# Reordered beginning of a one-core attention + MLP + expert kernel: cumulative-sum rows, value scaling, second head's maxima, table load and pair transfers

## The chip, the cores and the metric

The program runs on one core of a Trainium2 chip. The time is the device time of one execution in microseconds; the number to be forecast is the median over several executions.

## What is computed

Three stages follow each other. The first is causal attention with a decay over 4 batches x 8 heads, 576 positions and head dimension 64; the second a mixing and MLP block; the third an expert block with attention per expert. The change touches the first stage and its overlap with the second. Cut to that:

```python
# q, k, v: (4, 8, 576, 64), f: (4, 8, 576)
log_f = np.log(np.clip(f, 0.0001, 1.0))
cum = np.cumsum(log_f, axis=-1)
scores = scale * np.matmul(q, k.transpose(0, 1, 3, 2)) + (cum[..., :, None] - cum[..., None, :])
scores = np.where(causal, -1000000000.0, scores)
attn = np.exp(scores - np.max(scores, axis=-1, keepdims=True))
attn_out = (attn / (attn.sum(-1, keepdims=True) + 1e-09)) @ v
# second stage, x = heads of attn_out side by side, (4, 576, 512)
u = x + (xt @ U @ V).transpose(0, 2, 1)
y = u + np.maximum(u @ w_ch1, 0.0) @ w_ch2
```

## The kernel before

**Heads and pairs.** Heads go two by two: pair p holds heads 2p and 2p+1, and a batch is four pairs. `load_pair(p)` transfers q and k (`qkt`) and v (`vr`) from DRAM; `split_high(p)` casts q and k on ScalarE into the tiles `qa`, `ka` of the first head and `qb`, `kb` of the second; `split_low(p)` transfers the row of cumulative sums into rows 64 and 65 of `ka`, copies between the tiles by DMA, and subtracts the casts on GpSimd. There are two sets of head tiles, used by pairs in turn, and from pair 4 on one tile `qkt` and one `vr`.

**Per head.** `row_max` multiplies q by k into `ua` and `ub`, takes masked maxima on VectorE into the five columns of `mx`, turns `mx` on TensorE into `mt`, subtracts a constant into `mr` on VectorE, and sends `mr` by two DMAs (L186, L187) into row 66 of `qa`. Here this is called the row of that head. `scores` then multiplies all 67 rows into `sc` in two parts (u = 0, 1), takes the exponential on ScalarE (`pf`, L222), casts it (`ph`, L223), and subtracts on VectorE (`pl`, L224). `weighted_values` multiplies `ph`, `pl` by the values' parts `vh`, `vl`. The tiles `ua`, `ub`, `sc` share one PSUM pool of two buffers.

**Values.** `values(p)` is a generator in three steps: the absolute maximum `am` of `vr` (L251); its transpose `amt` and the power of two `ar` (L256 to L258); then the broadcast `rsp`, its reciprocal `rs` (L265), the scaling of `vr` (L270), the cast `vh` (L271) and the subtraction `vl` (L272).

**Cumulative sums.** `log_sums` reads f, takes Ln on ScalarE, scans on VectorE and leaves two rows per head in `chl`. It stores all of `chl` into `cdram` (L490). Pair 0 takes its rows from `chl`, all others read `cdram` (L548).

**First batch.** `first_batch` goes over heads h = 0 to 7. With the scores of head h go the maxima of head h+2, the row of head h+1, the weighted values of head h-1, and, where h is odd, the transfers of the pair after next (`next_inputs(p + 2)`). `mix(p)` forms `gp` and `g` (TensorE, ScalarE, VectorE L591), then `up` on TensorE, and stores the result for the MLP.

**Weights of the MLP.** `load_quarter_steps` reads pieces of the weights (`raw`), narrows them in three VectorE steps L308, L310, L311 with one ScalarE step L309 between the first two (into `wst`, one buffer), casts on ScalarE (L359, `w1h` or `w2h`) and subtracts on GpSimd (L360, `w1l` or `w2l`). A quarter has four pieces of `w1` and four of `w2`. `ffn_out` (L414) uses all four `w2` pieces of its quarter in each of its sums. MLP work is filled in between the heads from pair 5 on.

**What sets the order.** TensorE's instructions stand in the order of the code. On the other engines a scheduler orders the instructions when the program is built. Each engine then works through its list in that order; SyncE's list (SP) is the queue from which nearly all DMAs are issued. A DMA also waits on a completion count that an earlier DMA used.

The line numbers are those of the profile of before.

Of the kernel before, what the change touches and what calls it, by code (L numbers as in the profile page):

```python
# [8 lines left out]
F32 = mybir.dt.float32  # L9
# [5 lines left out]
AF = mybir.ActivationFunctionType  # L15
OP = mybir.AluOpType
# [3 lines left out]
B, H, S, D = 4, 8, 576, 64  # L20
# [15 lines left out]
PSCALE_LN = 8.0 * math.log(2.0)  # L36
# [9 lines left out]
ISC = 0.125  # L46
# [8 lines left out]
def f32(ap):  # L55
    return ap.bitcast(F32)
# [3 lines left out]
def kernel(  # L60
# [13 lines left out]
    nc = tc.nc  # L74
# [4 lines left out]
    def pool(name, bufs=1, side="left", space=None):  # L79
        kw = {} if space is None else {"space": space}  # L80
        if space is None:
            kw["side"] = side
            kw["reuse_waits"] = "tile"
        return tc.alloc_tile_pool(name=name, bufs=bufs, **kw)
# [6 lines left out]
    small = pool("small", 4)  # L91
# [43 lines left out]
    cdram = dram.tile([B * H, 2, S], F32, name="cdram")  # L135

    cur = {}
# [5 lines left out]
    def drain(gen):  # L143

        while True:
            try:
                next(gen)
            except StopIteration as end:
                return end.value

    def row_max(hb, mx, apart=False):


        qa, qb, ka, kb = hb
        ua = ps2.tile([P, 2, 512], F32, name="ua", tag="s2")
        for c0, c1 in ((0, HC), (HC, S)):
            nc.tensor.matmul(ua[:, c0 // HC, 0:HC], qa[0:66, M_LO[4]:S], ka[0:66, c0:c1],
                             start=True, stop=True)
        nc.vector.tensor_tensor_reduce(
            ua[:, :, 0:HC], ua[:, :, 0:HC],  # L160
            maskm[:].rearrange("p (c n) -> p c n", c=2), 1.0, NEG, OP.add, OP.max, mx[:, 4:5])
        if apart:
            yield
        ub = ps2.tile([P, 2, 512], F32, name="ub", tag="s2")
        where = {3: (0, 0), 0: (0, 448), 2: (1, 0), 1: (1, 320)}
        for t in (3, 2, 1, 0):
            bk, off = where[t]
            w = M_W[t]
            n = 64 if t == 0 else P
            nc.tensor.matmul(ub[0:n, bk, off:off + w], qa[0:66, M_LO[t]:M_LO[t] + n],  # L170
                             ka[0:66, 0:w], start=True, stop=True)
        for t in (3, 2, 1, 0):
            bk, off = where[t]
            w = M_W[t]
            n = 64 if t == 0 else P
            m0 = S - P if t == 0 else S - w
            nc.vector.tensor_tensor_reduce(  # L177
                ub[0:n, bk, off:off + w], ub[0:n, bk, off:off + w], maskm[0:n, m0:m0 + w], 1.0, NEG,
                OP.add, OP.max, mx[0:n, t:t + 1])
        yield  # L180
        mt = psf.tile([NT, P], F32, name="mt", tag="f")
        nc.tensor.transpose(mt[:], mx[:], ident[:])
        mr = small.tile([NT, P], F32R, name="mr", bufs=2)
        nc.vector.tensor_scalar(mr[:], mt[:], PSCALE_LN / ISC, None, OP.subtract)
        row = f32(qa[66:67, :])
        nc.sync.dma_start(row[:, 0:64], f32(mr[0:1, 0:64]))  # L186
        cur["last"] = nc.sync.dma_start(row[:, 64:S].rearrange("o (t p) -> o t p", p=P),  # L187
                                        f32(mr[1:NT, :]))
# [59 lines left out]
    def value_scale(vr):  # L248

        am = small.tile([P, 1], F32, name="am")  # L250
        nc.vector.tensor_reduce(am[:], vr, AX.XYZ, OP.max, apply_absolute_value=True)  # L251
        yield
        at_ = psf.tile([1, P], F32, name="amt", tag="f")
        nc.tensor.transpose(at_[:], am[:], ident[:])
        ar = small.tile([1, 1], F32, name="ar")
        nc.vector.tensor_reduce(ar[:], at_[:], AX.X, OP.max)  # L256
        nc.vector.tensor_scalar(ar[:], ar[:], 1.0e-30, None, OP.max)
        nc.vector.tensor_scalar(ar[:].bitcast(I32), ar[:].bitcast(I32), 0x7F800000, None,  # L258
                                OP.bitwise_and)
        yield  # L260

        rp = psf.tile([P, 1], F32, name="rsp", tag="f")
        nc.tensor.matmul(rp[:], ones1[:], ar[:].bitcast(BF16)[:, 1:2], start=True, stop=True)
        rs = small.tile([P, 1], F32, name="rs")
        nc.vector.reciprocal(rs[:], rp[:])  # L265
        return rs
# [209 lines left out]
    def log_sums():  # L476

        pa = cur["fu"].tile([P, 2, S], F32, name="pa", tag="uh")
        pb = cur["fu"].tile([P, 2, S], F32, name="pb", tag="ul")
        chl = cur["fu"].tile([P, 2, S], F32R, name="chl", tag="uh")  # L480
        fr, ones, cum = pa[0:B * H, 0, :], pa[0:B * H, 1, :], pb[0:B * H, 0, :]
        nc.sync.dma_start(fr, f)
        nc.vector.memset(ones, 1.0)
        nc.vector.tensor_scalar(fr, fr, 1.0e-4, 1.0, OP.max, OP.min)
        nc.scalar.activation(fr, fr, AF.Ln)
        nc.vector.tensor_tensor_scan(cum, ones, fr, 0.0, OP.mult, OP.add)
        nc.vector.tensor_scalar(chl[0:B * H, 0, :], cum, -1.0 / ISC, None, OP.mult)
        nc.vector.scalar_tensor_tensor(chl[0:B * H, 1, :], cum, -1.0 / ISC,
                                       f32(chl[0:B * H, 0, :]), OP.mult, OP.subtract)
        nc.sync.dma_start(cdram[:], f32(chl[0:B * H]))  # L490
        return chl

    cur["sums"] = log_sums()
# [20 lines left out]
    def pair_heads(p):  # L514
        return heads[2 * (p % 2)], heads[2 * (p % 2) + 1]
# [23 lines left out]
    def split_low(p):  # L539
        if p >= NPAIR:  # L540
            return
        qkt, vr = st_in[p]
        (qa, qb, ka, kb), (qa2, qb2, ka2, kb2) = pair_heads(p)
        tq, tk = qkt[:, 0, :], qkt[:, 1, :]
        for j in range(2):
            hb = pair_heads(p)[j]
            src = f32(cur["sums"][j:j + 1]) if p == 0 else cdram[2 * p + j]
            nc.sync.dma_start(f32(hb[2][64:66, 0:S]), src)  # L548
        nc.sync.dma_start(f32(qa2[lo_, :]), f32(qb2[hi_, :]))
        nc.sync.dma_start(f32(ka2[lo_, :S]), f32(kb2[hi_, :S]))  # L550
        nc.sync.dma_start(f32(qb[lo_, :]), f32(qa[lo_, :]))
        nc.sync.dma_start(f32(kb[hi_, :S]), f32(ka[lo_, :S]))
        nc.sync.dma_start(f32(kb2[lo_, :S]), f32(kb2[hi_, :S]))
        nc.gpsimd.tensor_tensor(qb[hi_, :], tq[lo_], f32(qa[lo_, :]), OP.subtract)
        nc.gpsimd.tensor_tensor(kb[lo_, :S], tk[lo_], f32(ka[lo_, :S]), OP.subtract)
        nc.gpsimd.tensor_tensor(qb2[lo_, :], tq[hi_], f32(qb2[hi_, :]), OP.subtract)
        nc.gpsimd.tensor_tensor(kb2[hi_, :S], tk[hi_], f32(kb2[hi_, :S]), OP.subtract)

    def values(p):
        if p >= NPAIR:  # L560
            return
        vr = st_in[p][1]
        st_rs[p] = yield from value_scale(vr[:])
        value_parts(vr[:], st_rs[p], *vhs[p % 2])

    def maxima(p, j, apart=False):
        if p < NPAIR:
            yield from row_max(pair_heads(p)[j], next_mx(), apart)

    def one(gen):  # L570

        next(gen, None)
# [50 lines left out]
    load_pair(0)  # L623
    split_high(0)
    split_low(0)
    del cur["sums"]
    drain(values(0))
    drain(maxima(0, 0))
    m_first = maxima(0, 1)
    one(m_first)  # L630
    load_pair(1)
    split_high(1)
    split_low(1)
# [57 lines left out]
    def next_inputs(p):  # L691
        load_pair(p)
        split_high(p)
        split_low(p)

    def pair_scores(p, j):
        st_p[p, j] = yield from scores(pair_heads(p)[j])

    def first_batch(m_next):

        mixing = vals = iter(())
        for h in range(2 * NP):
            p, j = divmod(h, 2)
            sc = pair_scores(p, j)
            m_last, m_next = m_next, maxima(p + 1, j, True)
            one(sc)
            one(m_next)
            if j == 0:  # L710
                xs[p] = sx.tile([P, NT, P], F32, name="x", bufs=2)
                vals = values(p + 1)
                one(vals)
            one(sc)
            one(m_last)
            if j == 1:
                next_inputs(p + 2)
            one(m_next)
            if j == 1:
                one(vals)  # L720
            if h > 0:
                attend(*divmod(h - 1, 2))
            if j == 0:
                one(vals)
                one(mixing)
            elif p > 0:
                mixing = mix(p - 1)
                one(mixing)
            if j == 1:
                weights_after(p)  # L730
        one(mixing)
        return m_next
# [475 lines left out]
```

## Time and profile before

| | |
|---|---|
| median of 3 runs | 910.22 us (908.41 to 911.0) |
| the profiled execution's own time | 908.8 us |
| its span, first to last instruction | 906.9 us |
| TensorE busy (PE) | 835.0 us, 92% |
| VectorE busy (DVE) | 540.5 us, 60% |
| ScalarE busy (ACT) | 431.3 us, 48% |
| GpSimd busy (POOL) | 298.7 us, 33% |
| mean granted TensorE clock | 0.967 |

A row of a timeline gives the start in us, the duration in us, the engine, the line, the operation, what it writes and reads, its shape, and in brackets how long its engine sat idle before it and who ended that idle time. SPq is the queue of SyncE, so its durations are those of issuing a DMA and not of the transfer. Rows of windows give busy time and number of instructions of each engine in a stretch, then the granted clock (1.00 is 2.4 GHz, 0.50 is 1.2 GHz), the share of the DMA engines and GB/s.

### The profile page before, as it was taken

What the parts mean: (1) busy time and instruction counts of PE and PEld (TensorE: products, weight loads), DVE (VectorE), ACT (ScalarE), POOL (GpSimd) and SP (SyncE); (2) the same over time, 40 slices, a digit from 0 to 9 for tenths busy, and PEclk for the clock granted to TensorE, in tenths of its full rate; (3) what the DMA queues carried; (4) which work ended last, traced back from release to release, by engine and by line L of the source; (5) the groups of instructions that cost most, each with busy time, mean ns of one, the idle gap of its engine ahead of it and who ended that gap; (6) DMA issues with size and microseconds to landing.
All of it is one profiled execution on the core that took longest, in us unless ns stands there. A gap on an engine that the chain in (4) does not pass through costs nothing.

```text
span 906.9 us, 19020 instructions
## 1 busy us (share of the span) xinstructions
PE 835.0 (92%) x7476; PEld 782.0 (86%) x7476; DVE 540.5 (60%) x1464; ACT 431.3 (48%) x836; POOL 298.7 (33%) x283
## 2 busy tenths in 40 slices
PE   2796798998999999989999999999999999989997
PEld 2685687887899989989999999999999898989775
DVE  6789887886676666642234443222223777787654
ACT  3667565565444554342145543322211575665553
POOL 9446464444423433011135243513202241311000
PEclk9989577999999999999999999999999999999998
DMA  6335465354333432103159663433203231311222
GB/s 189 110 102 163 136 198 168 108 155 121 123 114 88 134 109 59 42 15 119 53 185 330 218 223 116 120 108 116 80 26 92 54 86 40 87 41 35 73 89 71
DMA packets 68809, 101.94 MB, mean 112 GB/s; under 512 B 6640, under 2 KB 49456, under 8 KB 68720
## 3 DMA queue, kind: packets, MB, share of 16 engines
q1 hardware_dynamic: 64448, 92.47, 34.1%
q10 hardware_dynamic: 4272, 8.26, 2.6%
q8 instruction: 59, 0.97, 0.4%
q14 instruction: 30, 0.25, 0.1%
HBM read 60.33 MB, written 22.56 MB: 91 GB/s over the span
## 4 chain that ended last, share of the span: by engine, by line
PE 70%; DVE 13%; DMA 6%; ACT 6%; issue 3%; SPq 1%; POOL 1%; DVEq 0%; ACTq 0%; POOLq 0%
PE cps L414 19%; PE hps L399 18%; PE sc L213 8%; PE pq L913 4%; PE po L1025 3%; DVE pl L224 3%; PE pv L978 3%; PE av L240 3%; DVE ub L177 2%; PE ub L170 2%; PE gp L587 2%; DMA ust<-udram 2%; PE av L244 2%; PE av L242 2%; DMA vr<-in_v_dram 2%
## 5 line engine op out<-in xcount | busy, mean ns | idle before, releaser
L414 PE MATMUL cps<-hh,w2h 128*128 128x288 f32 x512 | 154.8, 303 | 4.7 <-ACT w2h L359 2.0
L224 DVE TENSOR_TENSOR pl<-pf,ph 128x576 f16<-128x576 f32 x144 | 122.8, 855 | 51.5 <-ACT ph L223 51.3
L414 PE MATMUL cps<-hh,w2l 128*128 128x288 f32 x512 | 151.3, 296 | 1.0 <-POOL w2l L360 1.0
L414 PE MATMUL cps<-hl,w2h 128*128 128x288 f32 x512 | 150.5, 294 | 0.0
L399 PE MATMUL hps<-uh,w1h 128*128 128x288 f32 x512 | 144.8, 304 | 0.1
L404 DVE SCALAR_TENSOR_TENSOR hl<-hps,hh 128x288 fp32r<-128x288 f32 x128 | 58.3, 455 | 140.6 <-ACT hh L403 140.5
L399 PE MATMUL hps<-uh,w1l 128*128 128x288 f32 x512 | 141.4, 298 | 0.0
L403 ACT ACTIVATE hh<-hps 128x288 fp32r<-128x288 f32 x128 | 52.4, 410 | 156.8 <-PE hps L399 156.6
L414 PEld LDWEIGHTS cps<-hh,w2h 128*128 128x128 f32 x512 | 96.3, 188 | 6.7 <-ACT w2h L359 2.7
L222 ACT ACTIVATE pf<-sc 128x576 f32<-128x576 f32 x144 | 83.8, 612 | 37.2 <-PE sc L213 34.6
L399 PEld LDWEIGHTS hps<-uh,w1h 128*128 128x128 f32 x512 | 97.4, 190 | 0.8 <-DVE yc L416 0.5
L399 PEld LDWEIGHTS hps<-uh,w1l 128*128 128x128 f32 x512 | 97.6, 191 | 0.0
L414 PEld LDWEIGHTS cps<-hh,w2l 128*128 128x128 f32 x512 | 96.2, 188 | 1.2 <-POOL w2l L360 1.2
L414 PEld LDWEIGHTS cps<-hl,w2h 128*128 128x128 f32 x512 | 96.2, 188 | 0.0
L223 ACT CAST ph<-pf 128x576 f16<-128x576 f32 x144 | 89.2, 637 | 1.5
L213 PE MATMUL sc<-qa,ka 67*128 67x288 f32 (+4 forms) x288 | 77.0, 327 | 13.7 <-DMA qa<-mr 6.9
L240 PE MATMUL av<-vh,ph 128*128 128x65 f16 x720 | 87.0, 202 | 1.5 <-DVE x L287 1.5
L399 PE MATMUL hps<-ul,w1h 128*128 128x288 f32 x512 | 88.3, 295 | 0.0
L177 DVE CUSTOM_DVE_ANT_0 ub<-ub,maskm 128x448 f32<-128x448 f32 x192 | 81.3, 424 | 8.5 <-PE ub L170 7.5
L242 PE MATMUL av<-vl,ph 128*128 128x64 f16 x720 | 85.7, 198 | 0.0
L244 PE MATMUL av<-vh,pl 128*128 128x65 f16 x720 | 85.4, 198 | 0.0
L240 PEld LDWEIGHTS <-ph 128*128 128x128 f16 x720 | 68.5, 101 | 9.9 <-DVE x L287 1.7
(182 smaller groups left out, 1955.2 us busy)
## 6 DMA issues: line engine op xcount, KB each, us to landing
raw<-in_w_dram SPq DMA_DIRECT2D x32, 512.0 KB
ust<-udram SPq DMA_DIRECT2D x20, 576.0 KB
qkt<-in_qk_dram SPq DMA_DIRECT2D x16, 576.0 KB
yc<-ydram SPq DMA_DIRECT2D x14, 576.0 KB
ydram<-yc SPq DMA_DIRECT2D x14, 576.0 KB
vr<-in_v_dram SPq DMA_DIRECT2D x16, 320.0 KB
udram<-ustage ACTq DMA_DIRECT2D x16, 288.0 KB
ydram<-ust SPq DMA_DIRECT2D x8, 576.0 KB
```

The costliest lines, as they stand in the source:

```text
L177: nc.vector.tensor_tensor_reduce(ub[0:n, bk, off:off + w], ub[0:n, bk, off:off + w], maskm[0:n, m0:m0 + w], 1.0, NEG, OP.add, OP.max, mx[0 ...
L213: nc.tensor.matmul(ps[:, bk, off:off + w], wa, xa, start=bk not in banks[:n], stop=bk not in banks[n + 1:])
L222: nc.scalar.activation(pfv, view, AF.Exp, scale=ISC)
L223: nc.scalar.copy(ph[:, o0:o0 + n], pf[:, 0:n])
L224: nc.vector.tensor_tensor(pl[:, o0:o0 + n], pf[:, 0:n], ph[:, o0:o0 + n], OP.subtract)
L240: nc.tensor.matmul(av[0:m, it, :], ph[0:k, c:c + m], vh[0:k, jt, :], start=first, stop=False)
L242: nc.tensor.matmul(av[0:m, it, 0:64], ph[0:k, c:c + m], vl[0:k, jt, :], start=False, stop=False)
L244: nc.tensor.matmul(av[0:m, it, :], pl[0:k, c:c + m], vh[0:k, jt, :], start=False, stop=last)
L399: nc.tensor.matmul(ph[:], wa[:, k, fs], xa[:, k, :], start=n == 0, stop=n == 3 * KT - 1)
L403: nc.scalar.activation(hh[:], ph[:], AF.Relu)
L404: nc.vector.scalar_tensor_tensor(hl[:], ph[:], 0.0, f32(hh[:]), OP.max, OP.subtract)
L414: nc.tensor.matmul(pc[:], wa[:, t, dsl], xa[:], start=n == 0, stop=n == 3 * FT - 1)
```

## The change

It has five edits. The store of `chl` into `cdram` leaves `log_sums` and is issued after the DMA that brings pair 0's second row of sums into `ka` (kept as `cur["row"]`). A one-column exponential, `soon`, follows the Ln, so that the exponential's table is loaded there. Of `values(0)` only the first two steps stand ahead of the maxima; its third step, and the first step of head 1's maxima, stand behind head 0's `mr` (kept as `cur["mr"]`). In `first_batch` the transfers, casts and copies of `next_inputs(p + 2)` may issue their SyncE instructions only after the row that was the last one issued when head h began.

```diff
-        nc.vector.tensor_scalar(mr[:], mt[:], PSCALE_LN / ISC, None, OP.subtract)
+        cur["mr"] = nc.vector.tensor_scalar(mr[:], mt[:], PSCALE_LN / ISC, None, OP.subtract)
...
+        soon = small.tile([B * H, 1], F32, name="soon", bufs=1)
...
         nc.scalar.activation(fr, fr, AF.Ln)
+        nc.scalar.activation(soon[:], fr[:, 0:1], AF.Exp)
...
-        nc.sync.dma_start(cdram[:], f32(chl[0:B * H]))
         return chl
...
-            nc.sync.dma_start(f32(hb[2][64:66, 0:S]), src)
+            cur["row"] = nc.sync.dma_start(f32(hb[2][64:66, 0:S]), src)
...
     split_low(0)
+    with tc.issue_after(cur["row"].ins):
+        nc.sync.dma_start(cdram[:], f32(cur["sums"][0:B * H]))
     del cur["sums"]
-    drain(values(0))
+    v_first = values(0)
+    one(v_first)
+    one(v_first)
     drain(maxima(0, 0))
     m_first = maxima(0, 1)
-    one(m_first)
+    with tc.issue_after(cur["mr"].ins):
+        one(m_first)
+    with tc.issue_after(cur["mr"].ins):
+        one(v_first)
     load_pair(1)
...
             sc = pair_scores(p, j)
+            row = cur["last"]
...
             if j == 1:
-                next_inputs(p + 2)
+                with tc.issue_after(row.ins):
+                    next_inputs(p + 2)
```

`issue_after(x)` orders each instruction of its block that runs on the engine of x behind x on that engine, without a semaphore.

On SyncE the queue of the beginning stood so before: the store, pair 0's rows of sums, copies, pair 1's rows out of `cdram`, copies, then head 0's row.

```order
L490 DMA cdram<-chl 32x1152
L548 DMA ka_137<-chl 2x1x576
L548 DMA ka_145<-chl 2x1x576
L549 DMA qa_143<-qb_144 64x576
L553 DMA kb_146<-kb_146 64x576
L548 DMA ka_153<-cdram 2x576
L549 DMA qa_159<-qb_160 64x576
L552 DMA kb_154<-ka_153 64x576
L553 DMA kb_162<-kb_162 64x576
L186 DMA qa_135<-mr 1x16x4
L187 DMA qa_135<-mr 1x4x128
L524 DMA vr<-in_v_dram 128x640
```

Now the store stands five places later, two copies ahead of the reads of `cdram`, which stand three and four places ahead of head 0's row:

```order
L549 DMA ka_138<-chl 2x1x576
L549 DMA ka_146<-chl 2x1x576
L554 DMA kb_147<-kb_147 64x576
L628 DMA cdram<-chl 32x1152
L550 DMA qa_160<-qb_161 64x576
L551 DMA ka_162<-kb_163 64x576
L549 DMA ka_154<-cdram 2x576
L549 DMA ka_162<-cdram 2x576
L552 DMA qb_153<-qa_152 64x576
L553 DMA kb_155<-ka_154 64x576
L186 DMA qa_136<-mr 1x16x4
L187 DMA qa_136<-mr 1x4x128
```

The store moved behind the rows of sums that it preceded, and closer to those that read it; the last copy for pair 1 moved behind head 0's row, and pair 2's `vr` further back.

On VectorE, at head 7, `g` of pair 2 stood before at the end of this stretch; `wst` is the second weight piece:

```order
L265 RECIPROCAL rs_1228<-rsp_1226 128x1
L270 TENSOR_SCALAR vr_922<-vr_922,rs_1228 128x640
L308 TENSOR_SCALAR wst_1295<-raw_1017 128x512
L224 TENSOR_TENSOR pl_1156<-pf_1184,ph_1155 128x512
L177 ISA ub_1217,mx2_96<-ub_1217,maskm_82 64x64
L224 TENSOR_TENSOR pl_1156<-pf_1188,ph_1155 128x512
L278 TENSOR_SCALAR den_1279<-av_1233,rs_950 128x5
L310 SCALAR_TENSOR_TENSOR wst_1295<-raw_1017,wst_1295 128x512
L311 SCALAR_TENSOR_TENSOR wst_1295<-raw_1017,wst_1295 128x512
L287 TENSOR_TENSOR x_1042<-av_1233,rn_1281 128x5x64
L591 TENSOR_TENSOR g_1290<-gp_1284,g_1290 32x128
```

Now:

```order
L224 TENSOR_TENSOR pl_1158<-pf_1165,ph_1157 128x576
L265 RECIPROCAL rs_1230<-rsp_1228 128x1
L310 SCALAR_TENSOR_TENSOR wst_1297<-raw_1019,wst_1297 128x512
L270 TENSOR_SCALAR vr_924<-vr_924,rs_1230 128x640
L278 TENSOR_SCALAR den_1281<-av_1235,rs_952 128x5
L311 SCALAR_TENSOR_TENSOR wst_1297<-raw_1019,wst_1297 128x512
L224 TENSOR_TENSOR pl_1158<-pf_1186,ph_1157 128x512
L224 TENSOR_TENSOR pl_1158<-pf_1190,ph_1157 128x512
L592 TENSOR_TENSOR g_1292<-gp_1286,g_1292 32x128
L177 ISA ub_1219,mx2_96<-ub_1219,maskm_82 64x64
L287 TENSOR_TENSOR x_1044<-av_1235,rn_1283 128x5x64
```

The piece's first step moved out of the stretch to a place ahead of it, and the last maximum and `x` moved behind `g`.

On VectorE, at pair 5, the eighth weight piece (the last of `w2` of the first quarter, `wst_1643`) stood before ahead of the two last `pl` of a head:

```order
L404 SCALAR_TENSOR_TENSOR hl_1867<-hps_1853,hh_1866 128x288
L308 TENSOR_SCALAR wst_1643<-raw_1634 128x512
L591 TENSOR_TENSOR g_1876<-gp_1870,g_1876 32x128
L310 SCALAR_TENSOR_TENSOR wst_1643<-raw_1634,wst_1643 128x512
L311 SCALAR_TENSOR_TENSOR wst_1643<-raw_1634,wst_1643 128x512
L224 TENSOR_TENSOR pl_1836<-pf_1892,ph_1835 128x512
L224 TENSOR_TENSOR pl_1836<-pf_1896,ph_1835 128x512
L308 TENSOR_SCALAR wst_1654<-raw_1650 128x512
L416 TENSOR_TENSOR ust_1550<-cps_1919,ust_1550 128x288
```

Now the seventh piece (`wst_1638`) stands there, and the eighth (`wst_1645`) behind them:

```order
L404 SCALAR_TENSOR_TENSOR hl_1869<-hps_1855,hh_1868 128x288
L308 TENSOR_SCALAR wst_1638<-raw_1627 128x512
L592 TENSOR_TENSOR g_1878<-gp_1872,g_1878 32x128
L310 SCALAR_TENSOR_TENSOR wst_1638<-raw_1627,wst_1638 128x512
L311 SCALAR_TENSOR_TENSOR wst_1638<-raw_1627,wst_1638 128x512
L224 TENSOR_TENSOR pl_1838<-pf_1894,ph_1837 128x512
L224 TENSOR_TENSOR pl_1838<-pf_1898,ph_1837 128x512
L308 TENSOR_SCALAR wst_1645<-raw_1636 128x512
L310 SCALAR_TENSOR_TENSOR wst_1645<-raw_1636,wst_1645 128x512
L311 SCALAR_TENSOR_TENSOR wst_1645<-raw_1636,wst_1645 128x512
L308 TENSOR_SCALAR wst_1656<-raw_1652 128x512
L416 TENSOR_TENSOR ust_1552<-cps_1921,ust_1552 128x288
```

From the fifth piece to the eighth, each stands about one place of a piece later; the ninth is where it was, so that from there on the lists of VectorE agree but for neighbours. On TensorE only the first 14 instructions changed places.

## Rows read from the trace of the kernel before

**Rows 1.** Windows, the first 20 us, and 144 to 154; columns as told above.

```profile
0.00:20.00 20.00, 4.47 (x16) 3.25 (x16) 13.25 (x34) 7.66 (x11) 18.18 (x41) 1.00 0.64 178
...
144.00:154.00 10.00, 9.39 (x71) 8.44 (x72) 9.54 (x24) 4.60 (x8) 4.02 (x3) 0.50 0.54 173
```

**Rows 2.** Timeline, SyncE's queue; columns as told above.

```profile
1.26 0.41 SPq L522 DMA_DIRECT2D qkt<-in_qk_dram  x1
...
7.28 0.58 SPq L490 DMA_DIRECT2D cdram<-chl  x1
...
11.59 0.58 SPq L548 DMA_DIRECT2D ka<-cdram  x2
...
17.54 0.56 SPq L186 DMA_DIRECT2D qa<-mr  x1
...
18.87 0.44 SPq L640 DMA_DIRECT2D ur<-in_u_dram  x1
```

**Rows 3.** Timeline, VectorE, the beginning.

```profile
10.44 0.82 DVE L251 TENSOR_REDUCE am<-vr 128x1 f32<-128x640 f32 x1 [1.47 <-DMA vr<-in_v_dram]
...
11.37 1.38 DVE L270 TENSOR_SCALAR vr<-vr,rs 128x640 f32<-128x640 f32 x1
12.68 0.75 DVE L159 CUSTOM_DVE_ANT_0 ua<-ua,maskm 128x576 f32<-128x576 f32 x1
...
17.24 0.27 DVE L184 TENSOR_SCALAR mr<-mt 5x128 fp32r<-5x128 f32 x1
...
21.35 1.45 DVE L308 TENSOR_SCALAR u<-ur 128x160 int32<-128x160 int32 x1 [2.59 <-DMA ur<-in_u_dram]
...
28.18 0.28 DVE L184 TENSOR_SCALAR mr<-mt 5x128 fp32r<-5x128 f32 x1 [1.55 <-PE mt L182]
```

**Rows 4.** Timeline, TensorE, the first scores of head 0.

```profile
19.99 0.58 PE L213 MATMUL sc<-qa,ka 67*128 67x288 f32 x1 [3.12 <-DMA qa<-mr]
```

**Rows 5.** Timeline, ScalarE: first cast, first exponential, pair 2's cast.

```profile
5.35 0.67 ACT L534 CAST qa<-qkt 64x576 fp32r<-64x576 f32 x1 [1.13 <-DMA qkt<-in_qk_dram]
...
22.83 0.34 ACT L309 ACTIVATE ur<-ur 128x160 f32<-128x160 f32 x1 [9.31 <-DVE u L308]
23.19 1.28 ACT L222 ACT_TABLE_LOAD   x1
24.49 0.65 ACT L222 ACTIVATE pf<-sc 128x576 f32<-128x576 f32 x1
...
27.40 0.67 ACT L534 CAST qa<-qkt 64x576 fp32r<-64x576 f32 x1 [1.56 <-PE sc L213]
```

**Rows 6.** Timeline, VectorE and TensorE, up to the wait for pair 2's g.

```profile
86.88 1.34 DVE L308 TENSOR_SCALAR wst<-raw 128x512 int32<-128x512 int32 x1
88.15 1.83 DVE L224 TENSOR_TENSOR pl<-pf,ph 128x512 f16<-128x512 f32 x1
...
94.03 0.58 PE L596 MATMUL up<-vs,g 96*128 96x256 f32 x1 [8.47 <-DVE g L591]
```

**Rows 7.** Timeline, all engines, around the first sum of `ffn_out`.

```profile
140.56 0.62 ACT L359 CAST w2h<-wst 128x512 fp32r<-128x512 f32 x1
...
141.32 1.26 POOL L360 TENSOR_TENSOR w2l<-wst,w2h 128x512 fp32r<-128x512 f32 x1 [0.69 <-ACT w2h L359]
141.73 2.00 DVE L224 TENSOR_TENSOR pl<-pf,ph 128x512 f16<-128x512 f32 x2 [2.36 <-ACT ph L223]
142.63 0.40 PE L414 MATMUL cps<-hh,w2l 128*128 128x288 f32 x1 [1.01 <-POOL w2l L360]
...
143.65 0.41 DVE L308 TENSOR_SCALAR wst<-raw 128x512 int32<-128x512 int32 x1
...
144.10 0.66 ACT L309 ACTIVATE raw<-raw 128x512 f32<-128x512 f32 x1 [1.89 <-DVE wst L308]
...
144.79 0.69 DVE L310 SCALAR_TENSOR_TENSOR wst<-raw,wst 128x512 int32<-128x512 int32 x1
...
145.52 1.80 DVE L311 SCALAR_TENSOR_TENSOR wst<-raw,wst 128x512 int32<-128x512 int32 x1
```

## The prediction

> **What bounds the kernel now.** I read the page first, then windows of each stretch, then the timelines. Over the whole run TensorE is busy 92%, but the change touches stretches where it isn't. In the first 20 us it is busy 4.47 us at a full granted clock [rows 1], so about 15.5 us of the span go to the way up to head 0's first scores. These start at 19.99 after waiting 3.12 for the row `mr` in `qa` [rows 4]: the reader should see that this is a chain (input, casts, maxima on VectorE, `mr`, two DMAs, scores) and that each link that gets shorter moves all that follows. The second stretch is the wait for pair 2's `g`: TensorE idles 8.47 us until 94.03, and VectorE ends it [rows 6]. The third is the first sum of `ffn_out`, where TensorE waits for the low part of the eighth weight piece until 142.63 [rows 7]. Behind that wait the granted clock stands at 0.50 (1.2 GHz) from 144 to 154 while TensorE is busy 9.39 of 10 us [rows 1]. On TensorE only the first 14 instructions change places, and from pair 6 on VectorE has nearly the list it had; so I take what is gained or lost by then as the result, since later waits are between engines that are all shifted alike.
>
> All sums are made against the profiled execution's 908.8 us (span 906.9). The median of the runs is 910.2, so 1.4 us are added at the end. A difference under 0.3%, 2.7 us, is about what a measurement of this kernel can't tell from none.
>
> **Part 1: the beginning, head 0's row.** VectorE made `mr` at 17.24 [rows 3]. Two things that stood ahead of it go behind it: the scaling of `vr`, 1.38, and head 1's first maximum, which is like head 0's 0.75 plus a read of its sum [rows 3]. Together that is at least 2.13, and about 2.4 with the reciprocal and that read; `mr` is then there at some 14.8. The reduction `am` of pair 1, which waits for `vr` until 10.44 [rows 3], stays ahead, so the chain can't gain more than what stands behind it.
>
> The row is not sent from VectorE, though. On SyncE it now stands behind the two reads of `cdram`, and these need the store. Before, the store was issued at 7.28 and the reads at 11.59 [rows 2], 4.3 later, with all the inputs still under way: `vr` of pair 1 had just come at 10.44 [rows 3]. Now the store comes behind the rows of `ka` and three copies. Its old place at 7.28 plus six issues of about 0.6 (the issue lengths in rows 2) makes about 11. How long it takes with the inputs out of the way no row shows. The nearest is `ur`, a transfer of like size on a calm queue: issued at 18.87, worked on at 21.35 [rows 2, 3], 2.5. The other end is the old 4.3. I take 2.5, since by 11 the inputs have landed: reads at 13.5, two reads and two copies until about 15.3, the row then instead of at 17.54 [rows 2]. So 2.2 are gained at the row; with 4.3 it is issued at 17.2 and 0.3 are gained.
>
> The extra exponential costs ScalarE a table load of 1.28 [rows 5] and a short instruction in a place where it idled 1.13 before the cast of `qa` [rows 5]. So that cast comes about 0.35 later. VectorE's wait for `vr` until 10.44 hides this; without that cover it would cost its 0.35.
>
> **Part 2: the table, and head 1's row.** Before, ScalarE's order was: narrow `ur` at 22.83, load the table at 23.19, exponential at 24.49 to 25.14, then the cast `ph` [rows 5]. Now the exponential stands ahead of `ur` and needs no load. `ph` then follows `ur` alone. `ur` was issued 1.33 behind the row [rows 2], now with one copy of 0.6 more in between: 15.3 + 1.33 + 0.6 = 17.2; plus 2.5 to land, 1.45 for VectorE's step [rows 3] and 0.34 for ScalarE's [rows 5], `ph` starts at 21.5 instead of 25.14: 3.65 earlier. Two casts of pair 2, from 27.40 to about 28.55, stood ahead of head 0's next exponentials and now stand behind them: 1.2 more [rows 5]. Sum of parts 1 and 2 by head 1's row: 4.9 (2.9 if the store takes 4.3, 5.5 if the table's place was wholly on the chain).
>
> One rule speaks against the low price of the load. The Trainium skill (ScalarE: Activation LUTs, What ACT_TABLE_LOAD costs) says that a switch to another set takes 1283 ns of load and about 1380 ns of drain, 2.66 us in all; by that the first cast would come about 1.7 later instead of 0.35. The row shows 1.28 for the load, and the exponential starts 0.02 after it ends, so no drain is seen behind it.
>
> **Part 3: pair transfers behind a row.** Pair 2's `qkt` was issued about when `ur` landed; now it stands behind head 1's row. That row's `mr` was made at 28.18 [rows 3], 4.9 earlier now, 23.3; issue at 23.6, and `qkt` 1.3 later, 24.9. Landing took 4.1 for pair 0's (issued at 1.26, cast at 5.35) [rows 2, 5], so the cast can start at 29.0. Head 1's scores start 2.45 after their row (17.54 to 19.99) [rows 2, 4], at 26.05; an estimated 2.2 for scores and exponential makes 28.2. The cast stands on ScalarE between that exponential and its `ph`, so `ph` waits up to 0.8. I take -0.7, from 0 (TensorE has head 2's maxima to do meanwhile) to -1.5. Later pairs' transfers I cost at nothing: a head's work lies between them and their casts, and it covers the 4.1; without that cover each would cost up to the same 0.8.
>
> **Part 4: pair 2's `g`.** One step of a weight piece, 1.34 [rows 6], leaves the stretch of VectorE ahead of `g`, and a maximum and `x` go behind it. The load of `g` has no other late input, so TensorE's wait of 8.47 shrinks: +1.3. Down to 0 if VectorE is only less crowded and not earlier; up to 3.0 if two `pl` take 1.00 each, as in [rows 7], and not 1.83 as in [rows 6].
>
> **Part 5: the eighth weight piece.** This is the loss. Before, its steps were done ahead of the two `pl` of 141.73, its high part was cast at 140.56, and its low part ended at 142.6 [rows 7]. Now the seventh piece has that place, and the eighth stands behind the `pl`, which end at 143.73. There the ninth piece ran before, and it shows the price: L308 0.41, ScalarE 0.66, L310 0.69 and L311 [rows 7]; the ninth's L311 took 1.80 beside other work, a like step 0.69. From the ninth's own rows L310 begins at 144.79 and ends at 145.48; plus 0.69 for L311, 0.62 for the cast and 1.26 on GpSimd [rows 7] is 148.1, with small gaps 148.2. TensorE needs it in the middle of its first sum and nothing else is in its list ahead: 148.2 - 142.63 = -5.6, with L311 at 1.80 -6.7. I take -5.6.
>
> Sum: 4.9 - 0.7 + 1.3 - 5.6 = -0.1, so 908.9 for the profiled execution and 910.3 for the median.
>
> **The rivals.** *The eighth piece comes in time.* For it: VectorE is behind by only one piece of some 3 us, and all that comes after 31 us may run ahead, since the heads' maxima start earlier than the weights. Against it: its steps stand in the list behind `pl`, and `pl` waited 2.36 for ScalarE's `ph` [rows 7], which needs that head's scores. Then 4.9 - 0.7 + 1.3 = 5.5: 904.7.
>
> *The wait in `ffn_out` brings a second slow stretch.* The wait grows from 1.01 [rows 7] to 6.6, towards the 8.47 at `g` [rows 6]. For it: the clock is at 0.50 behind the small wait already, and 9.39 us of work at 0.50 [rows 1] would be 4.7 at 1.00. If a deeper wait brings another ten such us, 4.7 are lost: -0.1 - 4.7 = -4.8, 915.0, slower than before. It decides from the point where the slow stretch behind the wait lasts some 6 us longer than before. Against it: it may just shift.
>
> *The row is held by the store (the change does not do what it says).* The store takes its old 4.3, the row is issued at 17.2, and the beginning gains 2.9: 2.9 - 0.7 + 1.3 - 5.6 = -2.1, 912.3. For it: SyncE has nothing but the reads behind the store and can't pass them. Against it: the old 4.3 fell in the crowded first 10 us.
>
> *The table switch costs twice its row,* another 1.3 ahead of the first cast, of which VectorE's wait for `vr` no longer hides all: -0.1 - 1.3 = -1.4, 911.6. The row of the load speaks against it; the Trainium skill's drain (ScalarE: Activation LUTs, What ACT_TABLE_LOAD costs) would be the reason.
>
> **How the numbers follow.** Forecast 910.3: 0.36. Piece in time, 904.7: 0.30. Second slow stretch, 915.0: 0.18. Row held, 912.3: 0.10. Table switch, 911.6: 0.06. Faster by over 0.3% is the second case, 0.30; slower is the third, 0.18; the others lie within, 0.52. The range leaves out the third case and a little of the edges: from 904.0, just below the piece in time, to 913.5, the row held with `ffn_out`'s -6.7 in place of -5.6.
>
> **What would show it.** In the profile after: head 0's row issued near 15.3 and its scores near 17.7; a table load next to Ln and none at head 0's exponential; head 1's `mr` near 23.3; the first cast of pair 2 waiting for `qkt` up to a us; the wait for `g` near 7.2; and in the first sum of `ffn_out` a wait for the low part of a piece that ends some 5 us after that head's `pl`. If the read of `cdram` ends its wait 4 us after the store's issue, the row is held and part 1 is wrong; if no wait in `ffn_out` exceeds 3 us, part 5 is wrong and the time is near 904.7; if the granted clock stays at 0.50 for over 15 us behind it, the slow case is true.

## The result, and the profile after

The changed kernel is slower: its median is 917.12 us over 20 runs, against 911.67 us for the kernel before in runs beside it; the ratio is 1.0065, interval 1.0042 to 1.0088. The forecast was 910.3 us with a range up to 913.5, so the time lies above the range. Two of the executions of the kernel before took 2631 and 2758 us, far off all the others, and don't count in the ratio. The profiled execution took 914.0 us (span 912.1) against 908.8 (906.9), 5.2 us more, nearly the difference of the medians, and both lie some 3 us under their kernel's median; so I set one trace against the other, though each is one execution.

The same instructions of TensorE can be followed through both traces, since it works through one list. The table follows one of each head, the transposition `mt` of its maxima (the starts are in us, the last row is the difference):

| head | 0 | 1 | 2 | 3 | 4 | 5 | 6 | 7 | 8 | 9 | 10 | 11 | 12 | 13 |
|---|---|---|---|---|---|---|---|---|---|---|---|---|---|---|
| before | 16.46 | 27.72 | 35.62 | 44.63 | 51.52 | 59.44 | 67.26 | 74.07 | 81.51 | 99.68 | 112.22 | 126.60 | 143.00 | 157.35 |
| after | 14.61 | 22.54 | 31.95 | 42.05 | 49.44 | 59.03 | 67.38 | 74.43 | 82.80 | 99.44 | 112.61 | 126.67 | 149.23 | 162.30 |
| after - before | -1.85 | -5.18 | -3.67 | -2.58 | -2.08 | -0.41 | +0.12 | +0.36 | +1.29 | -0.24 | +0.39 | +0.07 | +6.23 | +4.95 |

Three things are to be seen: a lead of 5.2 at head 1; that lead gone by head 6, long before the first sum of `ffn_out`; and 6.2 lost at once between heads 11 and 12. From there the difference stays between 4.6 and 7.2 to the end.

**The beginning** ends near where it was forecast. SyncE's queue in the timeline after (start, length of the issue):

```profile
11.02 0.58 SPq L628 DMA_DIRECT2D cdram<-chl  x1
...
13.50 0.57 SPq L549 DMA_DIRECT2D ka<-cdram  x2
...
15.33 0.56 SPq L186 DMA_DIRECT2D qa<-mr  x1
...
24.20 0.55 SPq L186 DMA_DIRECT2D qa<-mr  x1
...
25.55 0.37 SPq L523 DMA_DIRECT2D qkt<-in_qk_dram  x1
```

The store took 2.5 us from its issue to the reads, not the old 4.3, and head 0's row went out at 15.33 instead of 17.54 [rows 2]. ScalarE after:

```profile
4.23 1.28 ACT L487 ACT_TABLE_LOAD   x1
5.53 0.20 ACT L487 ACTIVATE soon<-pa 32x1 f32<-32x1 f32 x1
5.64 0.65 ACT L535 CAST qa<-qkt 64x576 fp32r<-64x576 f32 x1
...
19.31 0.65 ACT L222 ACTIVATE pf<-sc 128x576 f32<-128x576 f32 x1
...
29.22 0.67 ACT L535 CAST qa<-qkt 64x576 fp32r<-64x576 f32 x1 [0.33 <-DMA qkt<-in_qk_dram]
```

The load stands behind Ln, and the first exponential starts at 19.31, not 24.49 [rows 5]. TensorE after, the first scores of heads 0 and 1, the wait for pair 2's `g`, and the first sum of `ffn_out`:

```profile
17.77 0.58 PE L213 MATMUL sc<-qa,ka 67*128 67x288 f32 x1 [1.82 <-DMA qa<-mr]
...
26.77 0.58 PE L213 MATMUL sc<-qa,ka 67*128 67x288 f32 x1 [2.74 <-DMA qa<-mr]
...
93.78 0.58 PE L597 MATMUL up<-vs,g 96*128 96x256 f32 x1 [7.12 <-DVE g L592]
...
140.96 0.40 PE L414 MATMUL cps<-hh,w2h 128*128 128x288 f32 x1 [2.10 <-ACT w2h L359]
...
142.36 0.61 PE L414 MATMUL cps<-hh,w2l 128*128 128x288 f32 x1 [1.01 <-POOL w2l L360]
...
146.63 0.61 PE L414 MATMUL cps<-hh,w2h 128*128 128x288 f32 x1 [3.42 <-ACT w2h L359]
...
148.59 0.61 PE L414 MATMUL cps<-hh,w2l 128*128 128x288 f32 x1 [1.34 <-POOL w2l L360]
```

Some 1.4 of the lead of 5.2 belong to the trace of before. There VectorE's first step on `ur` began at 21.35, just after a subtraction on GpSimd (21.30), and took 1.45 [rows 3]. In four of the runs below the lists of these two engines agree with it up to there: the kernel before with the transfers' edit alone, with the early exponential alone, with the first weight piece a pair earlier, and with the light subtractions. In these the step began at 21.12 to 21.22, ahead of that subtraction, and took 0.24 to 0.33. In the one with the early weight piece:

```profile
21.19 0.24 DVE L308 TENSOR_SCALAR u<-ur 128x160 int32<-128x160 int32 x1 [2.45 <-DMA ur<-in_u_dram]
```

In the three without the early exponential, head 1's transposition came 1.33 to 1.37 earlier than in the trace of before. Against these the changed kernel leads by some 3.8 at head 1.

**The end of the stretch**: the sum waits four times, 7.87 us in all, for the high and low part of the seventh and then of the eighth piece, the last until 148.59. Before, it waited twice, 2.63 in all, and the low part of the last piece was there at 142.63 [rows 7]. VectorE after shows the place from which it comes:

```profile
141.46 2.00 DVE L224 TENSOR_TENSOR pl<-pf,ph 128x512 f16<-128x512 f32 x2 [2.12 <-ACT ph L223]
143.38 0.41 DVE L308 TENSOR_SCALAR wst<-raw 128x512 int32<-128x512 int32 x1
144.51 0.69 DVE L310 SCALAR_TENSOR_TENSOR wst<-raw,wst 128x512 int32<-128x512 int32 x1 [0.72 <-ACT raw L309]
145.24 0.69 DVE L311 SCALAR_TENSOR_TENSOR wst<-raw,wst 128x512 int32<-128x512 int32 x1
148.57 0.43 DVE L308 TENSOR_SCALAR wst<-raw 128x512 int32<-128x512 int32 x1 [2.63 <-POOL w2l L360]
```

The eighth piece begins when the `pl` end, and the ninth can't begin before GpSimd has read the eighth out of the one buffer `wst`: the pieces are a chain.

**The middle** is what the forecast did not see. Between VectorE's `mr` of head 1 and of head 7 there passed 46.93 us before and 52.71 after. The windows of just these stretches (before, then after; busy time of TensorE, its weight loads, VectorE, ScalarE, GpSimd), and under each the same with L224, the `pl`, alone:

```profile
28.18:75.11 46.93, 40.85 (x421) 35.98 (x421) 40.53 (x124) 33.31 (x62) 24.57 (x19) 0.89 0.37 99
...
28.18:75.11 46.93, 14.91 (x18) 0.89 0.37 99
```

```profile
23.64:76.35 52.71, 42.67 (x413) 37.78 (x412) 44.57 (x128) 33.58 (x62) 28.20 (x22) 0.94 0.44 126
...
23.64:76.35 52.71, 18.15 (x18) 0.94 0.44 126
```

Over these stretches 5.78 us are lost. VectorE was busy for 4.04 more, and 3.24 of these are the same 18 `pl`, which took 14.91 before and 18.15 after. One of them, head 3's first, before and after, with GpSimd beside it:

```profile
51.55 0.74 DVE L224 TENSOR_TENSOR pl<-pf,ph 128x576 f16<-128x576 f32 x1
```

```profile
52.26 1.40 POOL L556 TENSOR_TENSOR qb<-qkt,qb 64x576 fp32r<-64x576 f32 x1 [4.36 <-ACT qb L536]
```

```profile
49.01 1.85 DVE L224 TENSOR_TENSOR pl<-pf,ph 128x576 f16<-128x576 f32 x1
```

```profile
48.83 1.42 POOL L555 TENSOR_TENSOR qb<-qkt,qa 64x576 fp32r<-64x576 f32 x1 [7.22 <-ACT qa L535]
50.32 1.82 POOL L556 TENSOR_TENSOR kb<-qkt,ka 64x576 fp32r<-64x576 f32 x1
```

Before, `pl` is over (52.29) just as GpSimd's subtraction begins, and takes 0.74. After, the subtraction has begun at 48.83, and `pl` takes 1.85. It ends 0.61 after that subtraction does, as if it had waited for it. The Trainium skill (SBUF — State Buffer, SBUF: two separate sides) says that a VectorE operation with two inputs in this memory and a GpSimd operation that reads it hold one shared port in turn, and that the later one waits for the whole of the other. The trace agrees: 0.74 alone, 1.85 beside it.

The longer `pl` are not all of it. From `mr` of head 1 to `mr` of head 3 the time already grew from 16.91 to 18.87, 1.96 of the 5.78, while the six `pl` in between took no longer (before, then after, and under each the `pl` alone):

```profile
28.18:45.09 16.91, 13.34 (x96) 11.64 (x96) 14.02 (x43) 11.54 (x22) 8.85 (x8) 0.89 0.27 66
...
28.18:45.09 16.91, 4.63 (x6) 0.89 0.27 66
```

```profile
23.64:42.51 18.87, 13.95 (x94) 12.32 (x93) 14.20 (x45) 10.96 (x21) 10.86 (x10) 1.00 0.36 102
...
23.64:42.51 18.87, 4.55 (x6) 1.00 0.36 102
```

Ahead of this stretch, head 1's `mr` had already come 1.10 after its transposition and not 0.46. Head 0's `pl` stood ahead of it and took 2.03, beside a subtraction of pair 1 that began at 21.43; before, it took 0.76:

```profile
21.45 2.03 DVE L224 TENSOR_TENSOR pl<-pf,ph 128x576 f16<-128x576 f32 x1
```

Of the 1.96 in the stretch, 1.09 lie between the `mr` of heads 2 and 3, where TensorE became fast a head later. The first matmul of head 2's scores, before and after:

```profile
40.51 0.37 PE L213 MATMUL sc<-qa,ka 67*128 67x288 f32 x1 [1.30 <-DMA qa<-mr]
```

```profile
36.87 0.58 PE L213 MATMUL sc<-qa,ka 67*128 67x288 f32 x1 [0.70 <-DMA qa<-mr]
```

After, this matmul takes 0.37 to 0.40 from head 3 to head 7, and 0.61 at 95.71, where the granted clock is 0.50 (1.2 GHz). So the 1.00 that the windows give for the first heads, here and in [rows 1], can't be read as full speed. Between the transpositions of heads 2 and 3 TensorE was busy for 7.30 before and 8.66 after. The other 0.87, between heads 1 and 2, were not followed further.

### The profile page after: what moved, and what is told of

It is laid out like the page before. It is cut to its first block, busy times and chain, and to the rows that moved or that the text cites. A ratio compares the mean times of both kernels' runs of the same rounds, so it can differ in the third digit from the quotient of the medians.

```text
span 912.1 us, 19030 instructions
## 1 busy us (share of the span) xinstructions
PE 838.9 (92%) x7476; PEld 785.2 (86%) x7476; DVE 541.9 (59%) x1464; ACT 431.4 (47%) x837; POOL 301.8 (33%) x283
## 4 chain that ended last, share of the span: by engine, by line
PE 70%; DVE 12%; DMA 7%; ACT 4%; issue 4%; POOL 2%; SPq 1%; DVEq 0%; POOLq 0%; ACTq 0%
PE cps L414 19%; PE hps L399 19%; PE sc L213 8%; PE pq L923 4%; PE po L1035 3%; DVE pl L224 3%; PE pv L988 3%; DMA ust<-udram 3%; PE av L240 2%; DVE ub L177 2%; PE gp L588 2%; PE ub L170 2%; PE av L244 2%; PE av L242 2%; PE ua L157 1%
## 5 line engine op out<-in xcount | busy, mean ns | idle before, releaser
L224 DVE TENSOR_TENSOR pl<-pf,ph 128x576 f16<-128x576 f32 x144 | 128.7, 896 | 49.1 <-ACT ph L223 48.7
```

Of the source, the lines that this page charges most:

```text
L224: nc.vector.tensor_tensor(pl[:, o0:o0 + n], pf[:, 0:n], ph[:, o0:o0 + n], OP.subtract)
```

## Experiments

All ratios are to the kernel before, run beside each.

### Each part alone, and the change without one part

The kernel before with the pair transfers' edit alone (`issue_after(row.ins)` around `next_inputs`):

> The kernel before with the pair transfers' edit alone. Its list on VectorE puts the eighth weight piece behind the two pl too. Theory (that place costs 5.6 us wherever it comes from, and the beginning gains nothing here): ratio 1.004 to 1.009, with a wait of over 4 us more in the first sum of ffn_out. Rival (the loss of the changed kernel comes from the beginning's edits, not from this one): ratio 0.998 to 1.002.

Ratio 1.0095 (1.0072 to 1.0119), just above the theory's range. Head 1 came 1.33 early and head 7 2.56 late against the trace of before. Its first sum of `ffn_out` waits 2.03, 1.01, 4.51 and 0.80, 8.35 in all, against 2.63 before (1.62 and 1.01). The `pl` up to pair 2's `g` take 24.8 us (21.6 before). So this edit, without the beginning it was meant for, makes both losses: 3.9 between heads 1 and 7, and the longer wait.

The changed kernel without that edit:

```diff
-                with tc.issue_after(row.ins):
-                    next_inputs(p + 2)
+                next_inputs(p + 2)
```

> The changed kernel without the pair transfers' edit. Its list on VectorE still puts the eighth weight piece behind the pl. Theory 1 (the early lead of 5 us is used up because GpSimd's subtractions of the pairs now run beside pl, which take 26.5 us to pair 2's g instead of 21.6): the lead at pair 2's g is 2 to 4 us, pl take under 24 us up to there, and the late piece takes it all: ratio 1.000 to 1.004. Theory 2 (late transfers are not what uses the lead up): the lead at pair 2's g is under 1 us here too and the ratio stays at 1.005 to 1.008.

Ratio 1.0117 (1.0091 to 1.0143): slower still, above the ranges of both theories. The lead is not used up slowly here; it is gone at head 2 (+0.14), and the timeline shows why. SyncE's queue and TensorE's first scores of head 1:

```profile
24.53 0.35 SPq L523 DMA_DIRECT2D qkt<-in_qk_dram  x1
24.99 0.48 SPq L552 DMA_DIRECT2D qb<-qa  x1
25.52 0.58 SPq L186 DMA_DIRECT2D qa<-mr  x1
```

```profile
31.06 0.58 PE L213 MATMUL sc<-qa,ka 67*128 67x288 f32 x1 [7.11 <-DMA qa<-mr]
```

Head 1's row is issued at 25.52 behind a `qkt` of 576 KB, and its scores start 5.54 later; in the changed kernel it is 24.20 to 26.77, 2.57. So the edit on the transfers does keep the lead from head 1 to head 2. Without it the sum of `ffn_out` waits 9.57, and the `pl` up to `g` take 23.9.

The kernel before with the early exponential alone:

```diff
+        soon = small.tile([B * H, 1], F32, name="soon", bufs=1)
...
         nc.scalar.activation(fr, fr, AF.Ln)
+        nc.scalar.activation(soon[:], fr[:, 0:1], AF.Exp)
```

> The kernel before with the early exponential alone, whose lists else stand as before. Theory (VectorE is the bound from head 3 to pair 2's g, so what ScalarE gains at head 0 is used up by then): a lead of 1 to 2 us at head 1, under 1 us at pair 2's g, ratio 0.998 to 1.001. Rival (a lead is carried to the end): ratio 0.996 to 0.998 with the lead of 1 to 2 us unchanged at 300 us.

Ratio 1.0010 (0.9990 to 1.0030). A lead of 2.76 at head 1 was 0.70 at heads 6 and 7, and head 9 came 0.13 late. Some 1.4 of the 2.76 are the late step on `ur` in the trace of before, so the exponential itself gave about 1.4 at head 1, within the 1 to 2 expected. The time shows nothing of this lead.

### What the late pieces cost

The eighth piece ordered ahead of the `pl` of the changed kernel:

```diff
...
+                with (tc.issue_after(cur[gate].ins) if gate and u else nullcontext()):
+                    nc.vector.tensor_tensor(pl[:, o0:o0 + n], pf[:, 0:n], ph[:, o0:o0 + n],
+                                            OP.subtract)
```

> The changed kernel, with the last two pl of the first head of pair 5 ordered on VectorE behind the eighth weight piece, as they stood in the kernel before. Theory (the late eighth piece is the loss that stays): in the changed kernel TensorE starts that head's last low product some 5.6 us later than before, so here 5 to 6 us of the 5.2 us by which the span grew come back: time as before, ratio 0.997 to 1.003, and the weighted sum's first cps with the eighth low part waits under 2 us. Rival (the place of the piece does not matter, something later would be late instead): ratio stays at 1.005 to 1.008.

Ratio 1.0009 (0.9984 to 1.0034), as the theory had it, but its trace does not bear that out: the last waits of the sum are still 3.12 and 2.72, and head 12's transposition is 5.42 late. The profiled execution took 920.3 us, the longest of its 12 (median 914.1), so this pair of trace and median settles nothing.

So the whole chain was put back, by two orders earlier on:

```diff
+GATES = {(8, 0, 0): 2, (9, 0, 0): 4}
...
+                gate = GATES.get((which, u, o0))
+                with (tc.issue_after(cur["piece", 0, gate].ins) if gate is not None
+                      else nullcontext()):
+                    nc.vector.tensor_tensor(pl[:, o0:o0 + n], pf[:, 0:n], ph[:, o0:o0 + n],
+                                            OP.subtract)
```

> The changed kernel with two orders added on VectorE: head 8's first pl behind the third weight piece, head 9's first pl behind the fifth. With these the fifth to the eighth piece stand as in the kernel before, the eighth ahead of the two pl of head 10. Theory (the pieces pass one after another through one buffer, so what costs is that the whole chain from the fifth on is one place late, and ordering only the eighth ahead can't mend it): the waits of the first sum of ffn_out add up to under 4.5 us (7.9 in the changed kernel) and the lateness at the row behind it, 6.2, falls to 0 to 2: ratio 0.997 to 1.002. Rival (pl moved behind pieces are late in their place): lateness stays over 4, ratio 1.004 to 1.008.

Ratio 1.0005 (0.9977 to 1.0032). TensorE in the sum:

```profile
140.75 0.40 PE L420 MATMUL cps<-hh,w2h 128*128 128x288 f32 x1 [1.74 <-ACT w2h L365]
...
142.15 0.40 PE L420 MATMUL cps<-hh,w2l 128*128 128x288 f32 x1 [1.01 <-POOL w2l L366]
```

The waits are 2.75 in all, nearly as before, and head 12's transposition is 0.48 early instead of 6.23 late (head 11 was already 4.08 early). The profiled execution as a whole took 914.6 us all the same, 5.8 more than that of before. It loses this behind 340 us, where TensorE's list is the same: among others, the granted clock is 0.50 from 340.8 to 344.0 and from 405.7 to 408.9, where it is 1.00 before. So the trace shows that the waits are gone, and only the 12 executions show what that is worth. Nothing else of the change was edited: the late chain of pieces is the loss that stayed, and without it the change is worth nothing either way. One doubt is left: the run before this one has nearly the same ratio, and its one trace, of its longest execution, still has the long waits.

### What used up the lead

GpSimd's subtractions were cut to 64 columns in both kernels, which leaves out the rest of the low parts of q and k:

```diff
-        nc.gpsimd.tensor_tensor(qb[hi_, :], tq[lo_], f32(qa[lo_, :]), OP.subtract)
...
+        w = slice(0, S) if p < 2 else slice(0, 64)
+        nc.gpsimd.tensor_tensor(qb[hi_, w], tq[lo_, w], f32(qa[lo_, w]), OP.subtract)
...
```

> The kernel before with GpSimd's four subtractions per pair over 64 of 576 columns from pair 2 on; the rest of the low parts of q and k is left out, so it is a measure of GpSimd's share alone. Theory (pl is stretched only by GpSimd's work beside it): the pl up to pair 2's g take 17.5 to 20 us instead of 21.6. Partner of the next run.

> The changed kernel with the same subtractions cut to 64 of 576 columns from pair 2 on. Theory (the lead of the beginning is used up mainly by GpSimd's subtractions that moved beside pl): pl take 17.5 to 21 us instead of 26.5, and of the lead of some 5 us at head 1 against its partner, 2.5 or more are left at the maxima of head 7. Rival (the lead is used up by waits of another kind, late transfers or TensorE's own pace): under 1 us is left there, as in the changed kernel.

The 24 `pl` up to pair 2's `g`, by windows of L224, in the first and in the second kernel, and that `g`:

```profile
0.00:88.00 88.00, 18.95 (x24) 0.92 0.52 146
```

```profile
88.09 0.28 DVE L592 TENSOR_TENSOR g<-gp,g 32x128 fp32r<-32x128 f32 x1
```

```profile
0.00:84.80 84.80, 16.65 (x24) 0.94 0.52 146
```

```profile
84.90 0.28 DVE L593 TENSOR_TENSOR g<-gp,g 32x128 fp32r<-32x128 f32 x1
```

So `pl` fall from 21.6 and 26.4 to 18.95 and 16.65. The lead between the two is 3.1 at head 1 (the partner itself came 1.4 earlier there than the kernel before), 1.7 at head 7, under the 2.5 expected, and 3.2 at `g`, where the full kernels differ by 0.25. With GpSimd's work mostly away, 1.4 of the lead are lost from head 1 to head 7, and not 5.5 (of which up to 1.4 are the late step on `ur`). This fits GpSimd's work beside `pl` using up much of it, but does not prove it. The 3.2 at `g` is not a lead that was kept: between head 7 and `g` two `pl` of the partner took 1.43 and 1.70, and the same two in the second kernel 0.74 and 0.68. With other lengths the scheduler also ordered some steps differently, and each is one execution. Nor did the lead reach the end: the first took 901.76 us, the second 904.28.

### Pieces earlier

The changed kernel with the first weight piece prepared one pair earlier, run twice:

```diff
-WRATE = (0, 0, 1, 4, 4, 4, 3)
+WRATE = (0, 1, 1, 4, 4, 4, 2)
```

> The changed kernel with the first weight piece prepared a pair earlier (rates 0, 1, 1, 4, 4, 4, 2), so that the chain of pieces is a place ahead of before. Theory (the late chain is the loss): no wait over 2 us in the first sum of ffn_out; the piece's 2 us of VectorE work beside pair 2 cost up to 2 us there: ratio 0.996 to 1.002. Rival (VectorE is full there, and the earlier piece delays the maxima by as much): ratio 1.004 to 1.009.

> The changed kernel with the first weight piece a pair earlier once more, since its neighbours (one piece more, or without the beginning, or without the pair transfers' edit) came out at 1.003 to 1.004 and it alone at 0.994. Theory (the lists decide it, and this one has no late piece and keeps the beginning): 0.991 to 0.998 again. Rival (its place among its neighbours was the spread of a few executions): 0.999 to 1.005.

Ratios 0.9941 (0.9914 to 0.9968) and 0.9955 (0.9927 to 0.9983), medians 908.0 and 905.9 us: faster than both kernels, twice. Windows from 134 to 150 us, of before, of after, and of the second of these runs:

```profile
134.00:150.00 16.00, 11.98 (x96) 9.87 (x95) 12.88 (x34) 8.45 (x17) 6.84 (x5) 0.81 0.51 150
```

```profile
134.00:150.00 16.00, 8.06 (x47) 6.16 (x45) 9.50 (x22) 8.27 (x15) 7.56 (x5) 0.73 0.44 124
```

```profile
134.00:150.00 16.00, 13.38 (x127) 11.92 (x128) 11.75 (x39) 8.89 (x18) 6.49 (x4) 1.00 0.44 119
```

TensorE is busy 11.98, 8.06 and 13.38 of 16 us, at a granted clock of 0.81, 0.73 and 1.00. The sum of `ffn_out` has no wait for a piece there, the clock does not fall, and head 13 comes 4.97 earlier than before (2.26 in the first run's trace, an execution of 909.9 us, the tenth of its 12). The earlier piece has its price ahead of that in the second trace: heads 7 and 8 come 3.2 and 4.5 late where head 6 was 2.6 early; head 9 is 0.22 early again.

Is it the weights alone? The kernel before with the same rates:

> The kernel before with the first weight piece a pair earlier (rates 0, 1, 1, 4, 4, 4, 2) and nothing of the change. It tells what of the 0.994 of the changed kernel with the same rates is the beginning's and what the weights'. Theory (the beginning's edits are worth 2 to 5 us once no piece is late, so that both are needed): ratio 0.996 to 1.001, above the 0.994. Rival (the gain is the weights' alone, and the beginning's lead is used up): ratio 0.990 to 0.995.

Ratio 1.0034 (1.0006 to 1.0062): slower, above even the theory's range. The sum still waits 1.84 for a low part, in a trace of the longest of its 12 executions. So the gain needs the beginning too. Without the pair transfers' edit:

> The changed kernel without the pair transfers' edit, with the early piece. Theory (without that edit head 1's row queues behind transfers of 576 KB and the lead is gone at head 2, as seen without the early piece; with the piece in time the late-piece loss is gone too): ratio 0.997 to 1.003, first scores of head 1 within 1 us of before. Rival (the pair edit is what hurts, by GpSimd beside pl): ratio under 0.994.

Ratio 1.0041 (1.0013 to 1.0069), just above the theory's range. The lead is 4.91 at head 1 and gone at head 2 (+0.18), as without the early piece. With one piece more ahead:

> The changed kernel with two pieces more ahead (rates 0, 1, 2, 4, 4, 4, 1). Theory (one place is enough, a further one only loads VectorE where it is the bound, 2 us a piece): ratio 0.994 to 0.999. Rival (weights are still the bound behind pair 4): under 0.992.

Ratio 1.0027 (0.9998 to 1.0056), where 0.994 to 0.999 was expected. Its sum doesn't wait for pieces, the granted clock is 1.00 from 140 to 170, and yet the time is not better; so the sum without waits does not explain the whole gain with one piece. The profiled execution, 909.6, was the shortest of its 12 (median 914.1), so its trace tells little of the others, and why it is slower than with one piece stays open.

## Why the prediction was wrong

**Right, with two errors that cancel: parts 1 and 2.** The store's landing (2.5), the row (15.3, measured 15.33), head 0's scores (17.7, measured 17.77) and head 1's `mr` (23.3, measured 23.64) came as worked out; the lead of 4.9 was 4.54 at that `mr` and 5.18 at the transposition. But VectorE's step on `ur`, priced at 1.45 from the trace of before, took 0.24, so `ph` began at 20.37 and not at 21.5; and head 0's `pl`, which had no term, took 2.03 ahead of `mr`. That the sum came out is partly luck. The choice of the calm `ur` and not the old 4.3 as the nearest row was right. The Trainium skill's drain (ScalarE: Activation LUTs, What ACT_TABLE_LOAD costs) is not seen: the load ends at 5.51 and the exponential starts at 5.53. The rivals of the held row and of a dear table switch fall.

**Right in the number, not in the mechanism: part 4.** The wait for `g` is 7.12 instead of 8.47, 1.35 less; forecast 1.3. But 1.10 of these are TensorE coming to the wait later, at 86.66 and not at 85.56, and `g` itself came 0.25 earlier. Before and after:

```profile
93.69 0.28 DVE L591 TENSOR_TENSOR g<-gp,g 32x128 fp32r<-32x128 f32 x1
```

```profile
93.44 0.28 DVE L592 TENSOR_TENSOR g<-gp,g 32x128 fp32r<-32x128 f32 x1
```

From head 8's `mr` (83.78, then 83.11) VectorE needed 10.33 to `g` and not 9.91: the weight piece's step left this stretch, but one more `pl` fell into it, and the three took 4.88 where the two had taken 3.57. The agreement is luck.

**Right in mechanism and place, a little small: part 5.** The eighth piece's low part was awaited until 148.59; forecast 148.2. Head 12 came 6.2 late where head 11 had not been late, and 5.24 of that are longer waits in the sum: the forecast 5.6 was short by 0.6. That VectorE would have the piece in time was the largest rival, and it fell; putting the chain of pieces back moved the ratio from 1.0065 to 1.0005.

**Wrong: part 3 and the rule ahead of the parts.** Part 3 gave the transfers 0.7, the later ones nothing, since "a head's work lies between them and their casts, and it covers" the landing. The landing was covered, for the first cast all but 0.33 us. What was not costed is where the casts' followers go: GpSimd's subtractions moved with the casts to where `pl` stands, the 18 `pl` in between took 3.24 us more, and VectorE, busy for 40.53 of 46.93 us before, was 4.04 busier. What was lost from head 1 (-5.18) to head 7 (+0.36) is 5.5, not 0.7. The edit on the transfers alone lost 3.9 there. The rule that a lead stays, "since later waits are between engines that are all shifted alike", holds only where the durations stay, and here they changed, of `pl` and of TensorE's own matmuls. The early exponential alone shows the same without any moved transfer: 2.76 at head 1, nothing at head 9. How the 5.5 divide between the longer `pl` and the slower start is argued from the traces and not shown by a run of its own.

By the table the sum is 5.2 at head 1, -5.5 up to head 7, +0.6 up to head 9, -0.3 up to head 11, -6.2 at head 12 and +1.0 from there to the end: -5.2, what the spans show. Part 4's 1.35 is no term of it, since 1.10 of them were lateness of TensorE that the wait took up. The rival of a second slow stretch has the right sign and nearly the time, but not the cause. The granted clock is at 0.50 from 141.5 to 158.6 after and from 143.9 to 154.2 before, so the stretch is 6.8 longer, near the prediction's sign for this rival. But it begins earlier, inside the sum's waits: behind the last wait (148.59) 10.0 us of it are left, about the 10.3 of before, and head 13 is less late than head 12. A short one follows from 182.5 to 185.9, which before has not, and head 15 is 2.2 later there than head 14; by the end that is given back.

```profile
140.00:150.00 10.00, 3.27 (x11) 2.18 (x11) 4.68 (x8) 3.87 (x7) 5.01 (x4) 0.58 0.51 138
150.00:160.00 10.00, 10.00 (x80) 9.03 (x79) 7.59 (x23) 4.40 (x9) 2.62 (x2) 0.57 0.58 185
160.00:170.00 10.00, 10.00 (x110) 9.45 (x110) 9.04 (x26) 6.06 (x12) 6.28 (x4) 1.00 0.39 110
170.00:180.00 10.00, 9.26 (x101) 8.08 (x99) 6.69 (x19) 6.85 (x14) 2.70 (x2) 1.00 0.56 146
```

## What to carry to other kernels

Cost a moved transfer down to the last engine that it sets off: when it starts later, so do the casts and subtractions behind it, and what these stand beside may be slower for it. A lead won at the start is worth what the next bound engine can use of it, so ask which engine is waited for in the following stretch before carrying it to the end. Before pricing a step from one row, look whether another run with the same list has the same length: 1.45 for the step on `ur` was 0.24 to 0.33 in four others. And look in the order for the last member of a chain with one buffer, as the weight pieces here: one place later for a piece cost more than the whole beginning gained, and one piece earlier turned the change into a gain.

## What the runs showed of the hardware

A `pl` of 128x576 took 0.74 us alone and up to 2.03 beside a GpSimd subtraction, and GpSimd's own 1.40 grew to 1.82. A row of some 2 KB took 2.6 us from its issue to the matmul that needs it when it stood ahead of a `qkt` of 576 KB in the queue, and 5.5 when it was issued 1 us behind one. A load of the activation table was followed by the next activation after 0.02 us. The first matmul of a head's scores (67x288) took 0.58 us in the first heads and 0.37 to 0.40 later, from head 2 on in the trace of before and from head 3 on in that of after.
